# An order of work written out instruction by instruction, relu evictions over two PSUM banks, and a weight difference shared between two engines

## The chip, the cores and the metric

The kernel runs on one core of a Trainium2 chip. The metric is the time of one execution on the device, in microseconds. The core has five engines that run their own instruction streams and signal each other by semaphores: TensorE (PE, with PEld for its weight loads), VectorE (DVE), ScalarE (ACT), GpSimd (POOL) and SyncE (SP), whose queue issues DMAs here.

## The reference

Four batches of 12544 tokens of 128 channels go through an attention with 32 inducing points and then through a layer of two weight matrices, a maximum and an output matrix:

```
h   = mab(I, x)        # softmax over the 12544 tokens: 32 x 128 per batch
a   = mab(x, h)        # softmax over the 32 points: one row of 128 per token
g   = maximum(a @ w1, a @ w2)      # 50176 x 1024
out = g @ w_out                    # 50176 x 128, float32
mab(q, kv) = softmax(q @ kv.T / sqrt(128)) @ kv
```

## The kernel before, in words

A batch is 98 chunks of 128 tokens. Batch 0 is transposed by TensorE as it is loaded (the head, some 23 us); the other three are loaded by GpSimd's DMA queue while the batch before is computed (`load_x`, L223), transposed by SyncE's DMA queue (`transpose_x_dma`, L238), and reduced to h in steps that stand between the main work (`pool_scores` L393, `pool_turn` L437, `pool_accum` L442, then `small_rep`, `small_h`, `small_hwd`, `small_m1`). The last step of `pool_accum` issues the seven loads of the next batch.

The maximum is computed as max(a w1, a w2) = a w1 + relu(a (w2 - w1)). With e the unnormalised softmax of a token over 32 points and hwd = h (w2 - w1), the product for the relu has a depth of only 32, so TensorE does four of them beside each other, in four row groups. The main work on a block of up to 16 chunks, in four quarters of up to four:

- `stage` (L698): scores of the block by column-tiled products, and an exponential by ScalarE into the tile e2.
- `phase` (L1127): a visit. For up to four quarters, products of hwd and e2 (L1205) into a PSUM bank each, 512 columns a bank; with them, now and then, the products of m1 and e2 that add a w1 w_out. Then `relu_out` (L1095) evicts each bank to SBUF, by VectorE (L1107) or ScalarE (L1110) as a bit of the visit's second number says. The function can evict two neighbouring banks of one quarter at once (`holds`), which the order here never asks for.
- `final_one` (L974): one full product of 128 x 128 of relu and w_out (L989), 8 per chunk, added up in a bank per group of four chunks.
- `evict_group` (L1015): a group times the reciprocal of the softmax sum, by VectorE (L1024) or, for a few at the end, ScalarE (L1031), into one of six buffers `osbs`, which SyncE stores (L1049). The reciprocals come from `turn_e2` (L759: a DMA transpose of e2 and sums and a power by GpSimd, L776 and L780) or from `dens` (L804: small products and VectorE).

TensorE changes between full products, row tiling (the visits) and column tiling (stage, pool_scores, pool_accum). The order of this is a list of words (`ORDER`, L1229): `p4.9` is a visit of four with a mask of 9, a number is so many final products, `s` a stage, `g` a turn_e2, `x`, `c`, `t`, `a` steps of the next batch, `e`, `h`, `w`, `m` its small steps. Which bank, quarter and unit a word takes is decided while the program is built, by a model of the engines' times (`Clock`, L23) that also inserts dummy products (`dummies`, L617; `keep_busy`, L933) where it expects TensorE to wait.

In the head, w2 - w1 (`difference`, L622) is formed for columns 0 to 255 by VectorE and for the rest by GpSimd, w1 is cast to 16 bits (`cast_w1`), transposed by TensorE (`weights_2`, L635, with copies L646 and L649) and multiplied by w_out (`weights_3`, L654, L662).

The schedule within an engine is the program's order; the only waits are semaphores.

Of the kernel before, what the change touches and what calls it, by code (L numbers as in the profile page):

```python
# [16 lines left out]
INF = 1e9  # L17
# [90 lines left out]
class Quarter:  # L108


    def __init__(self, b, c0, w):
        self.b, self.c0, self.w = b, c0, w
        self.subs = {1: [1], 2: [2], 3: [2, 1], 4: [4]}[w]


class Block:


    def __init__(self, quarters, full=()):
        self.quarters = quarters  # L120
        self.width = max(qu.w for qu in quarters if qu)
        self.b = [qu.b for qu in quarters if qu][0]
        self.staged = None
        self.first = None
        self.divided = 0.0
        self.rp = None
        self.units = []
        self.done = {}
        self.relu = {}
        self.last_group = {}  # L130
        self.groups = []
        for q, qu in enumerate(quarters):
            jobs = []
            t0 = 0
            for w in qu.subs if qu else []:
                for u in range(2 * w):
                    jobs.append((q, t0, w, u))
                t0 += w
            self.units.append(jobs)
            if qu:  # L140
                self.groups.append(Group(self, [(q, t) for t in range(qu.w)], q in full))


class Group:
    def __init__(self, blk, chunks, full):
        self.blk, self.chunks, self.full = blk, chunks, full
        self.q = chunks[0][0]
        self.bank = self.ps = None
        self.started = self.linear = False
        self.order, self.parts = [], []  # L150
        for q, t0, w, u in blk.units[self.q]:
            jpb = 4 // w
            self.parts.append((t0, u))
            self.order += [(jpb * u + jj, t0 + t) for jj in range(jpb) for t in range(w)]
# [3 lines left out]
def kernel(  # L158
# [37 lines left out]
    relus = [big.tile([128, 2, 4096], F16, name=f"relus{q}", tag=f"relus{q}") for q in range(4)]  # L196
    relu1 = [big.tile([128, 1024], F16, name=f"relu1_{q}", tag=f"relu1_{q}") for q in range(2)]
    osbs = big.tile([128, NOUT, 4, C], F32, name="osbs", tag="osbs")

# [23 lines left out]
    def load_x(b, i, after=None):  # L223
        k0, n = parts[b][i]
        if after is not None:

            nc.gpsimd.tensor_copy(out=pace, in_=after)
        nc.gpsimd.dma_start(out=xn_at[b, i][:, 0:n, :], in_=xr[b, :, k0 : k0 + n, :])  # L228
        if b:
            issued = ck.on_pool(ck.pe, 0.55)  # L230
            if i == 0 and b > 1:
                ck.loading = issued - 0.55
            st[b]["ld", i] = ck.loading + 6.3 + 2.72 * i if b > 1 else 25.7 + 2.5 * i
# [4 lines left out]
    def transpose_x_dma(b, j):  # L238
        i, lo, n = turns_x[j]
        k0 = P1 * i + lo  # L240
        nc.sync.dma_start_transpose(xT_tiles[b % 2][:, k0 : k0 + n, :], xn_at[b, i][:, lo : lo + n, :])
        landed = ck.on_sp(st[b]["ld", i], "x7" if n == 7 else "x14")
        for k in range(k0, k0 + n):
            st[b]["T", k] = landed

    identity16 = consts.tile([128, 128], F16, name="identity16")
    head16 = relus[3][:, 0, :]
# [10 lines left out]
    wf = relus[0][:, 0, :].bitcast(F32)  # L258
    w1f, w2f = wf[:, 0:J], wf[:, J : 2 * J]
    w1s = relus[1][:, 0, :]  # L260
# [10 lines left out]
    with tc.manual_schedule(engines={ET.PE, ET.DVE, ET.Activation, ET.Pool, ET.SP}):  # L271

        xf = relus[2][:, 0, 0 : 256 * P1].bitcast(F32)
# [119 lines left out]
        def pool_scores(b, u):  # L393
            if u == 0:
                st[b]["es"] = smp.tile([128, NU], F32, name=f"es_{b}", tag="esu")
            bi, ps = bank([128, 512])
            ck.wait(ck.bank[bi], "p1")
# [10 lines left out]
            ck.feed(8)  # L408
            end = ck.run(0.226, "col")
# [3 lines left out]
            nc.scalar.activation(  # L413
                out=eu, in_=ps, func=AF.Exp, scale=scale, accum_out=st[b]["es"][:, u : u + 1]
            )
            ck.bank[bi] = ck.on_act(end, 0.575)
            st[b]["eu", u] = eu, ck.bank[bi]

        def pool_rest(b):

            bi, ps = bank([128, 512])
            ck.wait(ck.bank[bi], "p1")
# [8 lines left out]
            end = ck.run(0.029 * REST)  # L431
            et = etp.tile([128, P1, M], F16, name=f"et_{b}", tag="et")
            nc.scalar.activation(out=et[:, 0:REST, :], in_=ps[:, 0 : REST * M], func=AF.Exp, scale=scale)
            ck.bank[bi] = ck.on_act(end, 0.2)
            st[b]["et"] = et, ck.bank[bi]

        def pool_turn(b, u):  # L437
            eT = etp.tile([128, 8, 128], F16, name=f"eT_{b}_{u}", tag="eT", bufs=NEU)
            nc.sync.dma_start_transpose(eT, st[b]["pair", u // 2].rearrange("p v (j t) -> p (v j) t", j=4))
            st[b]["eT", u] = eT, ck.on_sp(st[b]["eu", u][1], "eT")  # L440

        def pool_accum(b, u):  # L442

            bi, ps = bank([128, 512])
            ck.wait(ck.bank[bi], "p1")
# [4 lines left out]
            if last:  # L450
                nc.vector.reduce_sum(out=acc[:, C : C + 1], in_=st[b]["es"], axis=AX.X)
                ck.on_dve(st[b]["eu", u][1], 0.1)
            eT = st[b]["eT", u][0]
            st[b]["sum", u] = True
# [12 lines left out]
            if last:  # L467
                et = st[b]["et"][0]
# [17 lines left out]
            ck.feed(64)  # L486
            end = ck.run(0.58 if last else 0.49, "col")
# [5 lines left out]
            ck.bank[bi] = ck.on_dve(end, 0.22)  # L493
            if last:
                st[b]["esrr"] = ck.bank[bi]
# [4 lines left out]
        def small_rep(b):  # L500

            bi, ps = bank([128, 512])
            ck.wait(ck.bank[bi], "p1")
            nc.tensor.matmul(out=ps[:, 0 : C + 1], lhsT=repd, rhs=st[b]["hacc"], start=True, stop=True)  # L504
            end = ck.run(0.28)
# [5 lines left out]
            ck.bank[bi] = st[b]["haccr"] = ck.on_dve(end, 0.45)  # L511

        def small_h(b):
            hT4 = smp.tile([C, 4, M], F16, name=f"hT4_{b}", tag="hT4")
            if b == 0:


                nc.vector.tensor_scalar(
                    out=hT4,
                    in0=st[0]["hps"][:, None, 0:M].broadcast_to((C, 4, M)),  # L520
                    scalar1=DOWN,
                    scalar2=None,
                    op0=ALU.mult,
                )
                st[b]["hT4r"] = ck.on_dve(st[0]["end"], 0.2)
                ck.bank[st[0]["hb"]] = st[b]["hT4r"]
                es = smp.tile([128, 1], F32, name="es_0", tag="es")
                nc.scalar.copy(out=es, in_=st[0]["eps"][:, 0:1])
                ready = ck.on_act(st[0]["end"], 0.1)
                st[b]["hT4"] = hT4.rearrange("c q m -> c (q m)")  # L530
                return es, ready
            bi, ps = bank([128, 128], F16)
            ck.wait(ck.bank[bi], "p1")
            nc.tensor.transpose(ps[:, 0:128], st[b]["h4"], identity16)
            end = ck.run(0.056)
            nc.vector.tensor_copy(out=hT4.rearrange("c q m -> c (q m)"), in_=ps[:, 0:128])
            ck.bank[bi] = st[b]["hT4r"] = ck.on_dve(end, 0.2)
            st[b]["hT4"] = hT4.rearrange("c q m -> c (q m)")
# [12 lines left out]
        def small_hwd(b, steps=(0, 1), vector=True):  # L551

            if b == 0:
                cuts = ((0, 256), (256, 512), (512, 1024))
            else:
                cuts = ((0, 512), (512, 1024))
            if 0 in steps:
                st[b]["hwd"] = smp.tile([128, J], F16, name=f"hwd_{b}", tag="hwd")
            hwd = st[b]["hwd"]
            for step in steps:  # L560
                lo, hi = cuts[step]
                w, sl = hi - lo, slice(lo, hi)
                bi, ps = bank([128, 512])
                ps = ps[:, 0:w]
                if b == 0 and step == 2:
                    n = int((w_of["w21", lo] + 0.05 - max(ck.pe, ck.bank[bi])) / 0.23)
                    if n > 0:
                        ck.wait(ck.bank[bi], "p1")
                        dummies(psall[:, bi, :], n)
                ck.wait(max(ck.bank[bi], st[b]["hT4r"], w_of.get(("w21", lo), 0.0) if b == 0 else 0.0), "p1")  # L570
                nc.tensor.matmul(out=ps, lhsT=st[b]["hT4"], rhs=w21[:, sl], start=True, stop=True)  # L571
                end = ck.run(0.215 * w / 512)
                if b == 0:
                    if vector:
                        nc.vector.tensor_scalar(  # L575
                            out=hwd[:, sl],
                            in0=ps,
                            scalar1=st[0]["rs"],
                            scalar2=1.0 / scale,
                            op0=ALU.mult,  # L580
                            op1=ALU.mult,
                        )
                    else:
                        nc.scalar.activation(out=hwd[:, sl], in_=ps, func=AF.Copy, scale=st[0]["rw"])
                elif step == 0:
                    nc.vector.tensor_copy(out=hwd[:, sl], in_=ps)
                else:
                    nc.scalar.copy(out=hwd[:, sl], in_=ps)
                if vector if b == 0 else step == 0:
                    ck.bank[bi] = ck.on_dve(end, 0.07 + w / 970.0)  # L590
                else:
                    ck.bank[bi] = ck.on_act(end, 0.06 + w / 1200.0)
                for piece in range(lo // 256, hi // 256):
                    st[b]["hw", piece] = ck.bank[bi]

        def small_m1(b):
# [726 lines left out]
```

## Time and profile before

| | us |
|---|---|
| median of 3 runs | 315.21 |
| lowest, highest | 314.35, 315.71 |
| span of the profiled execution (first to last instruction) | 312.9 |
| TensorE busy in it | 306.0 |
| ScalarE busy | 280.7 |
| VectorE busy | 273.1 |
| GpSimd busy | 122.6 |

The profiled execution is one execution of its own; its time by the device's clock is not given apart from its span, and the median of the runs lies 2.3 us above the span. Rows of groups read: line, engine, operation, output and inputs, shapes, count, then busy time, mean ns of one, and the engine's idle time before them with what ended it. Rows of a timeline read: start, duration, engine, line, operation, tiles, shapes, count. A matmul's end is modelled, so its row is longer than the time that it holds the array.

### The profile page before, as it was taken

To read this page: it belongs to the slowest core of one execution; us is meant where nothing else is said; L and a number is where in the kernel's file an instruction comes from. 1 tells how busy PE (TensorE), PEld (TensorE's weight loads), DVE (VectorE), ACT (ScalarE), POOL (GpSimd) and SP (SyncE) were. 2 spreads that over 40 slices of the span, in tenths; PEclk is the share of its full clock that TensorE was granted. 3 is DMA by queue.
4 is the path that set the end of the run, shared out by engine and by line. 5 is a ranking of instruction groups with operands and counts; after the bars stand their busy time and mean duration, and the time that the engine had idled before them with its cause. 6 is when DMAs were issued, how large, how long until landed. Compare 5 with 4: busy or idle time off the path is not lost.

```text
span 312.9 us, 12567 instructions
## 1 busy us (share of the span) xinstructions
PE 306.0 (98%) x5316; PEld 239.4 (77%) x5316; DVE 273.1 (87%) x485; ACT 280.7 (90%) x581; POOL 122.6 (39%) x183
## 2 busy tenths in 40 slices
PE   6999999999999999999999999999999999999996
PEld 2875777777877777778877887778778877788885
DVE  2458999999889999988999998999999899989894
ACT  3668999999989989999999999989999899998875
POOL 7374007910530006677500565139205743288000
PEclk9999999999999999999999999999999999999999
DMA  7999999999399999989699999993422522342223
GB/s 206 208 255 203 218 214 192 167 231 232 107 204 244 256 212 202 212 199 218 136 241 256 185 241 200 194 229 114 131 86 103 153 102 87 118 130 103 103 88 136
DMA packets 80793, 55.69 MB, mean 178 GB/s; under 512 B 62272, under 2 KB 65632, under 8 KB 80736
## 3 DMA queue, kind: packets, MB, share of 16 engines
q1 hardware_dynamic: 74768, 41.19, 56.5%
q0 software_dynamic: 5968, 13.70, 22.6%
q8 instruction: 41, 0.67, 0.9%
q14 instruction: 16, 0.13, 0.1%
HBM read 27.28 MB, written 25.69 MB: 169 GB/s over the span
## 4 chain that ended last, share of the span: by engine, by line
PE 94%; DMA 3%; DVE 1%; issue 1%; POOL 0%; ACT 0%; POOLq 0%
PE psall L989 61%; PE psall L1205 23%; DMA xn<-in_x_dram 3%; PE psall L712 2%; PE psall L458 1%; PE psall L399 1%; PE psall L309 1%; PE psall L371 1%; PE psall L325 1%; DVE relus L1107 1%; PE psall L571 1%; PE psall L504 0%; PE psall L362 0%; DVE hwd L575 0%; PE psall L819 0%
## 5 line engine op out<-in xcount | busy, mean ns | idle before, releaser
L1110 ACT ACTIVATE relus<-psall 128x512 f16<-128x512 f32 x468 | 239.2, 620 | 15.4 <-PE psall L1205 14.4
L1107 DVE TENSOR_SCALAR relus<-psall 128x512 f16<-128x512 f32 x308 | 195.5, 683 | 16.6 <-PE psall L1205 15.7
L989 PE MATMUL psall<-woutp,relus 128*128 128x128 f16 x3104 | 203.7, 220 | 0.0
L989 PEld LDWEIGHTS <-relus 128*128 128x128 f16 x3104 | 174.9, 98 | 33.1 <-issue 27.3
L1205 PE MATMUL psall<-e,hwd 32*128 32x512 f16 (+2 forms) x840 | 81.1, 362 | 0.0
L776 POOL TENSOR_TENSOR half<-ed 128x256 f32<-128x256 f16 (+2 forms) x22 | 13.4, 611 | 145.5 <-DMA ed<-e 145.5
L780 POOL TENSOR_TENSOR rd<-den,minus 128x16 f32<-128x16 f32 (+2 forms) x22 | 57.8, 2628 | 1.7
L1024 DVE TENSOR_TENSOR osbs<-psall,rd 128x512 f32<-128x512 f32 (+1 forms) x80 | 50.9, 637 | 4.3 <-PE psall L1205 1.3
L1205 PEld LDWEIGHTS <-hwd 32*128 32x128 f16 x880 | 27.9, 91 | 11.7 <-issue 2.3
L1205 PE MATMUL psall<-m,e 32*128 32x128 f16 x372 | 36.6, 216 | 0.0
L1205 PEld LDWEIGHTS <-e 32*128 32x128 f16 x372 | 22.2, 92 | 9.6 <-issue 2.0
L776 POOL TENSOR_TENSOR half<-half 128x32 f32<-128x32 f32 (+4 forms) x66 | 21.4, 324 | 5.2
L228 POOL DMA_DIRECT2D xn<-in_x_dram x32 | 17.8, 569 | 5.7 <-DMA xn<-in_x_dram 4.3
L1024 DVE TENSOR_TENSOR osbs<-psall,rp 128x512 f32<-128x512 f32 (+3 forms) x24 | 15.6, 649 | 0.5 <-PE psall L1205 0.4
L313 DVE COPY xT<-psall 128x512 f16<-128x512 f16 (+3 forms) x12 | 5.7, 485 | 8.6 <-PE psall L309 8.4
L413 ACT ACTIVATE eu<-psall 128x512 f16<-128x512 f32 x18 | 10.8, 612 | 0.3 <-PE psall L399 0.2
L725 ACT ACTIVATE e<-psall 128x512 f16<-128x512 f32 (+2 forms) x21 | 10.9, 574 | 0.1
L316 ACT COPY xT<-psall 128x768 f16<-128x768 f16 (+3 forms) x10 | 5.8, 576 | 4.6 <-PE psall L309 4.5
L309 PE MATMUL psall<-identity,xn 128*128 128x128 f16 x98 | 7.5, 219 | 1.5 <-DMA xn<-in_x_dram 1.0
L712 PE MATMUL psall<-xT,hT 128*32 128x512 f16 (+3 forms) x110 | 8.4, 362 | 0.0
L309 PEld LDWEIGHTS <-xn 128*128 128x128 f16 x98 | 5.5, 97 | 3.1 <-DMA xn<-in_x_dram 1.4
L399 PE MATMUL psall<-xT,inducingT 128*32 128x512 f16 x72 | 6.4, 381 | 0.0
(114 smaller groups left out, 129.8 us busy)
## 6 DMA issues: line engine op xcount, KB each, us to landing
out_dram<-osbs SPq DMA_DIRECT2D x90, 256.0 KB, 2.9
xn<-in_x_dram POOLq DMA_DIRECT2D x24, 448.0 KB, 9.9
out_dram<-osbs SPq DMA_DIRECT2D x10, 128.0 KB, 4.3
relus<-in_moe_w_dram POOLq DMA_DIRECT2D x4, 256.0 KB, 5.7
xn<-in_x_dram POOLq DMA_DIRECT2D x4, 224.0 KB, 10.3
xT<-xn SPq DMA_TRANSPOSE x33, 4.3
relus<-in_x_dram SPq DMA_DIRECT2D x1, 512.0 KB, 4.0
relus<-in_x_dram SPq DMA_DIRECT2D x1, 384.0 KB, 4.4
```

The source lines that it names most:

```text
L228: nc.gpsimd.dma_start(out=xn_at[b, i][:, 0:n, :], in_=xr[b, :, k0 : k0 + n, :])
L309: nc.tensor.transpose(ps[:, j, :], xn[:, g + j, :], identity16)
L413: nc.scalar.activation(out=eu, in_=ps, func=AF.Exp, scale=scale, accum_out=st[b]["es"][:, u : u + 1])
L712: nc.tensor.matmul(out=ps[32 * q : 32 * (q + 1), 128 * t : 128 * (t + n)], lhsT=hq, rhs=xT[:, c : c + n, :], start=True, stop=True, tile_p ...
L725: nc.scalar.activation(out=blk.e2[:, 0 : 128 * wd], in_=ps[:, 0 : 128 * wd], func=AF.Exp, scale=st[0]["rs"] if blk.b == 0 else scale,)
L776: nc.gpsimd.tensor_tensor(out=dst, in0=cur[:, :, 0:n], in1=cur[:, :, n : 2 * n], op=ALU.add)
L780: nc.gpsimd.tensor_tensor(out=rp[:, 0:wd, :].rearrange("p t q -> p (t q)"), in0=den[:, 0 : 4 * wd], in1=minus1[:, 0 : 4 * wd], op=ALU.pow,)
L989: nc.tensor.matmul(out=g.ps[lo:hi, 128 * c : 128 * (c + 1)], lhsT=relu[:, lo:hi], rhs=woutp[:, jb, :], start=not g.started, stop=(state["m ...
L1024: nc.vector.tensor_mul(osb[:, 0:m, :], g.ps[:, 0 : m * C].rearrange("p (s c) -> p s c", s=m), g.blk.rp[:, t0 : t0 + m, q : q + 1].broadcas ...
L1107: nc.vector.tensor_scalar(out=dst, in0=src, scalar1=0.0, scalar2=None, op0=ALU.max)
L1110: nc.scalar.activation(out=dst, in_=src, func=AF.Relu)
L1205: nc.tensor.matmul(**seq.pop(0))
```

## The change

The order is written out in full (`PLAN`): the list says for each visit which quarters it takes, into which bank each goes and which engine evicts it, and for each other step its bank. `p01+12v26a37a` is a visit: quarter 0 into bank 1 and quarter 1 into bank 2, both evicted by one VectorE instruction (`+`), quarter 2 into bank 6 and quarter 3 into bank 7, each evicted by ScalarE. `l` and `L` add the m1 products of the open or the held group, digits behind a colon give the order of the products, `o` opens a group in a bank, `d` is so many final products. The model of the engines no longer decides anything but in the head. Its description says that the list has 157 visits and that no transpose is issued during a burst of loads.

```
-    relus = [big.tile([128, 2, 4096], F16, ...) for q in range(4)]
+    slots = big.tile([128, 64, 512], F16, name="relus", tag="relus")
...
+        def relu_out(parts, vector):
+            if len(parts) == 2:
+                (a, ba), (z, bz) = [(home[1] + unit[2], bi) for home, unit, bi, _, _ in parts]
+                assert a < z and ba < bz
+                dst = slots[:, a : z + 1 : z - a, :]
+                src = psall[:, ba : bz + 1 : bz - ba, :]
+            else:
...
+            if vector:
+                nc.vector.tensor_scalar(out=dst, in0=src, scalar1=0.0, scalar2=None, op0=ALU.max)
+            else:
+                nc.scalar.activation(out=dst, in_=src, func=AF.Relu)
...
-        difference(nc.gpsimd, 512, J, 22.9, 1.25)
+        difference(nc.gpsimd, 512, 768, 22.9, 0.64)
...
+        difference(nc.vector, 768, J, 23.1, 0.34)
...
-        s p4.9 s p2.2 H1 V W p2.2 p4.2 14 m0 p3.1 4 p3.2 4 p3.3 15 p4.2 6 x1.0 2 p3.6 15 p4.8 13 p4.5 14
+        s6 p00+11a25v:12012000 s7 H2.0.0 p14v V3.6 p15v p00a p11v32v x1.0 p27a o4.1 d4.1 W6.0 p03a20a35a o7 d4
...
-        EVICT = "...000101101"
+        EVICT = "...000011010"
```

The relu results of all quarters lie in one tile, so that two banks of different quarters, neighbours or not, can go by one instruction with a stride between their halves. The list has 138 such evictions. The digit 0 or 1 of `EVICT` gives a group's eviction to VectorE or ScalarE. The steps of the head up to the second `difference` are as before, as are the loads and the number of products; the two kinds of reciprocals are shared out differently by one block.

More of the change, by code (lines that the diff above doesn't have):

```diff
@@ L412, in pool_scores, with pool_rest @@
             eu = st[b]["pair", u // 2][:, u % 2, :]
[L413 to L422, printed above, removed]
+            nc.scalar.activation(out=eu, in_=ps, func=AF.Exp, scale=scale, accum_out=st[b]["es"][:, u : u + 1])
+        def pool_rest(b, bi):
+            ps = main_bank(bi)
             for j in range(REST):
@@ L558, in small_hwd @@
+        def small_hwd(b, step, bi, scalar):
+            if step == 0:
                 st[b]["hwd"] = smp.tile([128, J], F16, name=f"hwd_{b}", tag="hwd")
[L559 to L594, printed above, removed]
@@ L933, in keep_busy @@
[L933 to L950 removed]
+        held = []
@@ new lines, with open_group, products @@
+        evicted = [0]
+        def open_group(bi, ahead=0):
+            g = groups[state["g"] + ahead]
+            assert not g.started and g.ps is None
+            g.bank, g.ps = bi, main_bank(bi)
+        def products(n, ahead=0):
+            g = groups[state["g"] + ahead]
+            home, _ = relu_home(g.blk, g.q)
+            w4 = g.n
+            more = max(0, n - (g.n * NJB - g.mm))
+            for _ in range(n - more):
+                jb, t = g.order[g.mm]
+                g.mm += 1
+                nc.tensor.matmul(
+                    out=g.ps[:, 128 * t : 128 * (t + 1)],
+                    lhsT=home[:, 128 * (jb * w4 + t) : 128 * (jb * w4 + t + 1)],
+                    rhs=woutp[:, jb, :],
+                    start=not g.started,
+                    stop=(g.mm == g.n * NJB and g.linear),
```

845 lines of the change are left out of this document (326 added, 519 removed).

## The prediction

> **What bounds the kernel now.** I read the page's shares and its chain of waits first, then what TensorE waited for, then the order of its work in a short window.
>
> ```profile
> span 312.9 us, 12567 instructions
> PE 306.0 (98%) x5316; PEld 239.4 (77%) x5316; DVE 273.1 (87%) x485; ACT 280.7 (90%) x581; POOL 122.6 (39%) x183
> PE 94%; DMA 3%; DVE 1%; issue 1%; POOL 0%; ACT 0%; POOLq 0%
> ```
>
> The chain that ended last lies on TensorE for 94%, although VectorE and ScalarE are busy for 87% and 90%. A busy engine need not delay another. Who did delay TensorE is in its list of waits (us in total, times, longest), six rows of which two below 0.5 us are left out:
>
> ```profile
> PE psall L840 <- DVE ones_q L292: 1.2, 1, 1.2
> PE psall L309 <- DMA xn<-in_x_dram: 1.0, 2, 0.8
> PE psall L662 <- DVE relus L646: 0.5, 1, 0.5
> PE psall L309 <- DVE xn L836: 0.5, 1, 0.5
> ...
> ```
>
> All of them belong to the first 27 us. After that TensorE waits for no relu eviction that this view shows. So the change can win two things only: less work on TensorE, and the few waits of the head. Relief of VectorE and ScalarE wins nothing by itself.
>
> What TensorE's work costs besides multiplying is seen in its timeline (start, duration, line, count):
>
> ```profile
> 150.56 0.40 PE L1205 MATMUL psall<-e,hwd 32*128 32x512 f16 x4
> 150.89 0.95 PE L989 MATMUL psall<-woutp,relus 128*128 128x128 f16 x14
> 151.78 0.40 PE L1205 MATMUL psall<-e,hwd 32*128 32x512 f16 x4
> 153.86 0.60 PE L1205 MATMUL psall<-e,hwd 32*128 32x512 f16 x5
> 154.41 0.84 PE L989 MATMUL psall<-woutp,relus 128*128 128x128 f16 x12
> 80.13 1.84 PE psall L989 x31
> 244.05 2.29 PE psall L989 x39
> ```
>
> The last two rows are pieces of the chain: 8 products more take 0.45 us, so one costs 56 ns. The run of 14 lasts from 150.89 to 151.78, 0.89 us, of which 14 x 56 ns are 0.78; the entry costs 0.106 us. A visit (the four-row-group products of L1205 between two such runs) of 512 columns deep takes 0.33 us, one of 1024 deep (153.86 to 154.41) 0.55; 512 columns are thus 0.22 us and its entry is 0.11 us.
>
> **The change part by part.** Counts are from the order of both built programs.
>
> *Fewer visits.* Runs in row tiling go from 165 to 158, full runs from 163 to 157, column-tiled ones from 25 to 26: 12 entries fewer, 12 x 0.106 = **-1.27 us**, all on the path. The products themselves are the same 3136 of L989 and 1262 of L1205; the columns of the deepest row group, summed over visits, grow by 256 (+0.11 us), and four small sum products go (about as much). These two cancel.
>
> *The head.* The new order takes 512 of the 1024 columns of w2 - w1 apart: 256 to GpSimd, 256 to VectorE, and scales hwd before two of the relus.
>
> ```profile
> 22.85 1.26 POOL L623 TENSOR_TENSOR w<-relus 128x512 f16<-128x512 f32 x1
> 20.84 0.89 POOL L623 TENSOR_TENSOR w<-relus 128x256 f16<-128x256 f32 x1 [0.63 <-DMA relus<-in_moe_w_dram]
> 20.71 0.42 DVE L623 TENSOR_TENSOR w<-relus 128x256 f16<-128x256 f32 x1
> 23.63 1.89 DVE L1107 TENSOR_SCALAR relus<-psall 128x512 f16<-128x512 f32 x3 [0.46 <-PE psall L1205]
> 24.16 0.61 PE L619 MATMUL psall<-warm 128*128 128x512 f16 x2
> 25.26 0.81 PE L619 MATMUL psall<-warm 128*128 128x512 f16 x3
> 25.43 0.74 DVE L575 TENSOR_SCALAR hwd<-psall,rs 128x512 f16<-128x512 f32 x1
> 26.09 0.41 DVE L646 COPY relus<-psall 128x512 f16<-128x512 f16 x1
> 26.56 0.62 PE L662 MATMUL psall<-woutp,relus 128*128 128x128 f16 x8 [0.48 <-DVE relus L646]
> ```
>
> Five dummies (512 columns, 0.22 us each) and the 0.48 stall are 1.58 us in which TensorE did nothing useful, waiting for VectorE's row of three relus, hwd and the copy L646. In the new order GpSimd ends its 256 columns at 22.85 + 0.89 = 23.74, VectorE its own, behind the scale at 23.02, near 23.6; then come on VectorE one relu (to 24.3), hwd (its product ends near 24.35, so to 25.1), one relu (25.65), the copy (26.05). L662 starts at about 26.05 in place of 26.5, and TensorE comes to it at about 26.0, since a visit and four products now stand ahead in place of the dummies. I take **-1.5 us**; no row shows the new order, so the ends are 0 (another engine ends as late as L646 did) and -2.0.
>
> *Two-bank evictions* replace 186 single ones on ScalarE by 93, and 90 on VectorE by 45.
>
> ```profile
> L1110 ACT ACTIVATE relus<-psall 128x512 f16<-128x512 f32 x468 | 239.2, 620 | 15.4 <-PE psall L1205 14.4
> L725 ACT ACTIVATE e<-psall 128x512 f16<-128x512 f32 x18 | 10.0, 613 | 0.1
> L725 ACT ACTIVATE e<-psall 128x128 f16<-128x128 f32 x2 | 0.6, 296 | 0.0
> L1024 DVE TENSOR_TENSOR osbs<-psall,rd 128x512 f32<-128x512 f32 x68 | 46.5, 683 | 2.3 <-PE psall L1205 1.1 <-ACT e L725 0.4 <-PE psall L989 0.3
> L1024 DVE TENSOR_TENSOR osbs<-psall,rd 128x256 f32<-128x256 f32 x8 | 3.3, 417 | 1.6 <-ACT osbs L1031 1.1 <-ACT relus L1110 0.6
> 149.41 4.51 ACT L1110 ACTIVATE relus<-psall 128x512 f16<-128x512 f32 x9
> ```
>
> Instructions overlap: nine on ScalarE last 4.51 us, so one follows another after (4.51 - 0.62)/8 = 0.486 us, not 0.62; on VectorE (1.89 - 0.68)/2 = 0.60. An element costs (613 - 296)/384 = 0.83 ns on ScalarE and (683 - 417)/256 = 1.04 ns on VectorE. A pair should then take a pitch of 0.486 + 0.42 = 0.91 for 0.97, and 0.60 + 0.53 = 1.13 for 1.20: 93 x 0.06 + 45 x 0.07 = 9 us freed on two engines, nothing on the path. From the row durations the pair would save more, 620 - 424 = 0.20 and 683 - 533 = 0.15; that is the upper end, 25 us; the lower end is a pair as dear as two singles. Neither moves the sum while TensorE does not wait.
>
> [...]
>
> A pair frees its banks late, though, and the new list reuses banks sooner. A single eviction needs 0.17 us from the end of streaming (a 0.38 us product row less its 0.21 of streaming), 0.62 or 0.68 for itself and some 0.05 for the signal. I laid all evictions' distances, in TensorE work at the prices above, from the last product into a bank to the next one that overwrites it, beside this need: 4 places of before fall short, by 0.14 us together, and 14 of the new list, by 0.94, the worst 0.25. The difference, **+0.8 us**, I take as added wait (bounds 0 and 1.5: queues ahead of an eviction come on top). Behind such a wait stands all of TensorE's stream, and VectorE and ScalarE wait for it in turn.
>
> *The rest.* The last eviction moves to VectorE: **-0.1** by the rows below. One block more is transposed by DMA and summed by GpSimd (39% busy, some 5 us, hidden). The order of the DMAs is a rival's matter.
>
> ```profile
> 309.86 0.37 ACT L1031 ACTIVATE osbs<-psall,rd 128x128 f32<-128x128 f32 x1 [0.62 <-PE psall L963]
> L1024 DVE TENSOR_TENSOR osbs<-psall,rd 128x128 f32<-128x128 f32 x4 | 1.2, 288 | 0.4 <-issue 0.2 <-PE psall L1205 0.2
> ```
>
> **Sum:** -1.27 - 1.5 + 0.8 - 0.1 = -2.07. The span of 312.9 becomes 310.8; around it lie 315.21 - 312.9 = 2.3 us (median less span), which stay. **Forecast 313.1 us**, 0.7% less.
>
> **The rivals.**
>
> *Given back in the evictions' queues (314.4).* In stretches of 5 us of TensorE's work, the list hands ScalarE more than 5 us (at the pitches above) in places that sum to 5.8 us, before 2.8; VectorE 4.1 against 1.3. Before, such peaks cost no wait in the list above; twice the peaks, in pairs that hold two banks, may cost 1.3 us more than I took. For it: one stretch of 10 us holds 10.8 us of ScalarE's. Against it: the totals fall. [...]
>
> *Pairs as dear as two singles (314.6).* The lower end above: ScalarE keeps its 264 us and loses the slack in a shorter span, and each of the 14 short places waits 0.1 us more: +1.5. Nothing here speaks for it but that no pair was measured.
>
> *Transposes into the loads: it does not do what it says (317, slower).* Of the change it is said that no transpose is issued during a burst of loads. The queues say otherwise.
>
> ```profile
> 84.77 3.82 POOL L228 DMA_DIRECT2D xn<-in_x_dram  x7 [0.31 <-PE psall L989]
> 86.03 20.22 SPq L1049 DMA_DIRECT2D out_dram<-osbs  x10
> 106.34 4.30 SPq L241 DMA_TRANSPOSE xT<-xn  x3
> 153.99 17.25 SPq L1049 DMA_DIRECT2D out_dram<-osbs  x8
> out_dram<-osbs SPq DMA_DIRECT2D x6, 256.0 KB, 7.8
> out_dram<-osbs SPq DMA_DIRECT2D x15, 256.0 KB, 3.0
> xT<-xn SPq DMA_TRANSPOSE x2, 8.3
> xT<-xn SPq DMA_TRANSPOSE x11, 4.3
> DMA to landing us min/median/max: 1.6/2.9/9.7
> ```
>
> Before, ten stores (one in 2.2 us) pass between the loads' issue and the first transpose, and eight in the third batch. While loads land a store takes 7.8 us, else 3.0 (windows 84 to 107 and 107 to 150); two transposes issued in the first burst took 8.3, else 4.3; the last row is all stores'. The new list lets six stores pass and four, then come four and two transposes, with stores behind them: near 97 us, ten before the loads are through. A store behind four transposes lands after 9.7 + 4 x 1.43 (the issue pitch of the row of three) = 15.4 us. There are 108 stores in 280 us and six buffers, 15.6 us a round: beyond this VectorE waits for a buffer, and TensorE for VectorE. If a transpose there costs 0.5 us more, the wait is 2 us in each of two bursts: +4. Against it: the first transpose stands behind stores that themselves land only when the loads are through.
>
> [...]
>
> **How the numbers follow.** Forecast 0.56, queues 0.22, pairs 0.10, transposes 0.12. A measurement here tells 0.5% (1.6 us) from no change: faster means below 313.6. That is the forecast's case and a little of the others, 0.58; same 0.24 (most of queues, half of pairs); slower 0.18. Range: at the low end all head and no added wait, 315.2 - 1.27 - 2.0 - 0.1 = 311.8, less 0.8 for small waits that no row names: 311.0; at the high end the transposes' 317.
>
> **What would show it.** Visits: 158 runs of products in row tiling at the same 0.33 and 0.55 us. Head: L662's successor (L607) starting near 26.0, without dummies ahead of it. Pairs: a row of 128x1024 near 1.04 us on ScalarE and 1.21 on VectorE. Short banks: waits of TensorE for relu evictions, 0.25 us at most, below 1 us in all; several us of them mean the queues. Stores landing later than 15 us and VectorE's L871 waiting for them mean the transposes. The prediction is wrong if TensorE's share falls below 97%.

## The result, and the profile after

| | before | after |
|---|---|---|
| median of 17 runs, us | 314.78 | 313.99 |
| lowest, highest | 314.35, 315.9 | 313.17, 315.54 |
| span of the profiled execution | 312.9 | 311.4 |

The ratio of after to before is 0.9977, 95% interval 0.9966 to 0.9987: 0.7 us faster, a third of the 2.07 of the sum. That the forecast of 313.1 comes within 0.9 us of 313.99 is luck: its base was the median of three runs, 315.21, and seventeen have 314.78. From that base the sum gives 312.7, 1.3 us too low.

The first lines of the page of after, with the shares of its chain:

```profile
span 311.4 us, 12499 instructions
...
PE 305.2 (98%) x5306; PEld 239.8 (77%) x5306; DVE 271.0 (87%) x443; ACT 275.5 (88%) x485; POOL 127.0 (41%) x189
...
PE 89%; DMA 6%; POOL 2%; DVE 2%; issue 1%; POOLq 0%; DVEq 0%
```

TensorE is as busy as before (98%), but its share of the chain fell from 94% to 89%. DMA and GpSimd have taken what it lost, but a link of the chain counts with its whole duration, not with the wait that it caused: 2% of the span, 6.5 us, are the landing of w1 and w2 at 14 to 21 us, ahead of the change. What the new order made TensorE wait for is in its list of waits, and it is small (us in total, times, longest; rows that before had too are left out):

```profile
PE psall L535 <- POOL w L576: 0.3, 1, 0.3
...
PE psall L430 <- DMA eT<-eu: 0.2, 1, 0.2
```

L576 is the difference w2 - w1, L535 the product hwd that reads it, L430 an accumulation that reads a DMA transpose. Neither was in the list of before. The evictions by shape (count, busy us, mean ns of one, idle time):

```profile
L902 ACT ACTIVATE relus<-psall 128x512 f16<-128x512 f32 x280 | 150.9, 608 | 14.4 <-PE psall L956 13.4 <-ACT relus L902 0.3
L900 DVE TENSOR_SCALAR relus<-psall 128x512 f16<-128x512 f32 x220 | 141.8, 684 | 15.2 <-PE psall L956 14.5
L902 ACT ACTIVATE relus<-psall 128x1024 f16<-128x1024 f32 x93 | 93.7, 1029 | 7.2 <-PE psall L956 6.7 <-ACT et L410 0.4
...
L900 DVE TENSOR_SCALAR relus<-psall 128x1024 f16<-128x1024 f32 x45 | 54.9, 1219 | 3.7 <-PE psall L956 3.4
```

A pair lasts 1.03 and 1.22 us, as forecast (1.04, 1.21).

**One execution is not the typical one.** In result and profile together, time and span lie 1.75 us apart (313.17 and 311.4; another run 314.15 and 312.4), not the 2.3 that the prediction took. So the profiled run of before, 312.9, was one of 314.7 us, a typical one, and that of after is the fastest of its seventeen. Part of the reason is in its head: the first product of the sums (of the softmax, L504, before L544) starts at 21.13 us, against 21.52 before, where nothing has been changed yet; TensorE had waited 0.4 us for loads, against 1.0. The difference of the two spans, 1.5 us, must therefore not be explained as it stands. The first experiment is the same kernel again.

**How the waits below are counted.** I add up TensorE's own work at the prediction's prices (56 ns a product, 0.105 us an entry, and for each column of the deepest row group some 0.42 ns, as dummies of 512 columns follow each other after 0.215 us: before, one lasts 0.38 us and three last 0.81) and subtract it from the real start of each product. Where this difference is flat, TensorE runs at its price; where it steps up, it waited. The price of an entry is put in here, not measured; it has an experiment of its own, the last. Two numbers are used: the *head stretch*, from the first product of the sums to the first of w1 w_out (L504 to L607, before L544 to L662), and the *waits after the head*, the growth from 30 us to the end.

### The profile page after: what moved, and what is told of

Same layout as the page of the kernel before. It is cut to its first block, busy times and chain, and to the rows that moved or that the text cites. A ratio compares the mean times of both kernels' runs of the same rounds, so it can differ in the third digit from the quotient of the medians.

```text
span 311.4 us, 12499 instructions
## 1 busy us (share of the span) xinstructions
PE 305.2 (98%) x5306; PEld 239.8 (77%) x5306; DVE 271.0 (87%) x443; ACT 275.5 (88%) x485; POOL 127.0 (41%) x189
## 4 chain that ended last, share of the span: by engine, by line
PE 89%; DMA 6%; POOL 2%; DVE 2%; issue 1%; POOLq 0%; DVEq 0%
PE psall L836 60%; PE psall L956 22%; DMA xn<-in_x_dram 3%; DMA relus<-in_moe_w_dram 2%; PE psall L644 2%; PE psall L430 1%; PE psall L385 1%; DVE relus L900 1%; DMA eT<-eu 1%; POOL xn L219 1%; POOL w L576 1%; PE psall L546 0%; PE psall L469 0%; DVE m1bd L565 0%; PE psall L852 0%
## 5 line engine op out<-in xcount | busy, mean ns | idle before, releaser
L902 ACT ACTIVATE relus<-psall 128x512 f16<-128x512 f32 (+1 forms) x373 | 234.0, 713 | 21.6 <-PE psall L956 20.1
L900 DVE TENSOR_SCALAR relus<-psall 128x512 f16<-128x512 f32 (+1 forms) x265 | 194.4, 775 | 18.9 <-PE psall L956 17.8
L956 PE MATMUL psall<-e,hwd 32*128 32x512 f16 (+2 forms) x840 | 80.2, 362 | 0.2
L697 POOL TENSOR_TENSOR half<-ed 128x256 f32<-128x256 f16 (+2 forms) x23 | 14.1, 612 | 141.8 <-DMA ed<-e 141.7
L701 POOL TENSOR_TENSOR rd<-den,minus 128x16 f32<-128x16 f32 (+2 forms) x23 | 60.7, 2639 | 1.8
L871 DVE TENSOR_TENSOR osbs<-psall,rd 128x512 f32<-128x512 f32 (+2 forms) x85 | 53.9, 636 | 4.2 <-issue 1.1
L956 PE MATMUL psall<-m,e 32*128 32x128 f16 x372 | 35.5, 217 | 0.0
L697 POOL TENSOR_TENSOR half<-half 128x32 f32<-128x32 f32 (+4 forms) x69 | 22.3, 323 | 5.4
L871 DVE TENSOR_TENSOR osbs<-psall,rp 128x512 f32<-128x512 f32 (+3 forms) x20 | 12.7, 641 | 0.4 <-PE psall L956 0.3
L385 PE MATMUL psall<-xT,inducingT 128*32 128x512 f16 x72 | 6.0, 382 | 0.0
```

The lines of the kernel that those rows point to most:

```text
L697: nc.gpsimd.tensor_tensor(out=dst, in0=cur[:, :, 0:n], in1=cur[:, :, n : 2 * n], op=ALU.add)
L701: nc.gpsimd.tensor_tensor(out=rp[:, 0:wd, :].rearrange("p t q -> p (t q)"), in0=den[:, 0 : 4 * wd], in1=minus1[:, 0 : 4 * wd], op=ALU.pow,)
L871: nc.vector.tensor_mul(osb[:, 0:n, :], g.ps[:, 0 : n * C].rearrange("p (s c) -> p s c", s=n), blk.rp[:, 0:n, q : q + 1].broadcast_to((128, ...
L900: nc.vector.tensor_scalar(out=dst, in0=src, scalar1=0.0, scalar2=None, op0=ALU.max)
L902: nc.scalar.activation(out=dst, in_=src, func=AF.Relu)
L956: nc.tensor.matmul(**seq.pop(0))
```

## The experiments

| run | median us | ratio to before, 95% | head stretch us | waits after the head us |
|---|---|---|---|---|
| before | 314.78 | | 5.04 | 3.66 |
| after, first profile | 313.99 | 0.9977 (0.9966 to 0.9987) | 4.87 | 5.05 |
| r1_same_again | 314.13 | 0.9978 (0.9964 to 0.9992) | 5.05 | 5.55 |
| r2_singles | 315.55 | 1.0021 (1.0011 to 1.0032) | 5.50 | 6.92 |
| r3_head_by_gpsimd | 314.28 | 0.9977 (0.9966 to 0.9989) | 5.26 | 5.91 |
| r4_deadlines | 314.10 | 0.9969 (0.9956 to 0.9982) | 4.70 | 5.27 |
| s1_old_order_split_head | 315.50 | 1.0015 (0.9998 to 1.0032) | 5.04 | 3.90 |
| s2_deadlines | 313.62 | 0.9967 (0.9949 to 0.9985) | 5.57 | 4.79 |
| s3_m1bd_by_gpsimd | 313.96 | 0.9980 (0.9959 to 1.0001) | 5.55 | 4.39 |
| s4_head_by_vector | 313.72 | 0.9957 (0.9942 to 0.9972) | 4.55 | 5.36 |
| t1_three_repairs | 312.96 | 0.9931 (0.9911 to 0.9952) | 4.55 | 4.38 |
| t2_cast_later | 313.08 | 0.9939 (0.9918 to 0.9961) | 4.53 | 4.63 |
| t3_banks | 312.90 | 0.9936 (0.9913 to 0.9958) | 4.56 | 4.74 |
| u1_twelve_more_entries | 316.22 | 1.0044 (1.0024 to 1.0064) | 4.84 | 4.55 |

Each ratio is to runs of the kernel before made beside that run, so ratios compare better than medians. The last two columns are of the one profiled execution. The profile of s3_m1bd_by_gpsimd shows a granted clock of 0.7 in its fourth slice of 40 (23.5 to 31.3 us), where the eight products of w1 w_out last 0.98 us, against 0.62 in after; its head is not used.

### The same kernel again

> The changed kernel once more, for a second profile. Theory A (the execution profiled first began with loads that landed early, and is not typical): TensorE's first product for the sums of the head starts near 21.5 us as in the kernel before, not at 21.1, the span is about 312.2, and from 30 us on TensorE falls behind its own work by about 1.4 us more than in the kernel before. Theory B (that execution is typical, and its 1.5 us less in the span is what the change gives): 21.1 us again and a span near 311.4.

Theory A. The sums start at 21.40, the span is 312.3, and the waits after the head exceed those of before by 1.9 us, not 1.4. The start is a matter of the execution: in the fourteen profiles it lies between 21.13 and 21.74. The timeline of its head (start, duration, engine, line; DVE is VectorE, POOL GpSimd):

```profile
21.40 0.38 PE L504 MATMUL psall<-es,relus 128*128 128x1 f32 x2 [0.18 <-ACT es L488]
...
23.02 1.14 DVE L576 TENSOR_TENSOR w<-relus 128x256 f16<-128x256 f32 x1
23.08 0.75 POOL L576 TENSOR_TENSOR w<-relus 128x256 f16<-128x256 f32 x1
...
24.21 0.39 PE L535 MATMUL psall<-w,hT 128*128 128x512 f16 x1 [0.49 <-DVE w L576]
...
26.45 0.62 PE L607 MATMUL psall<-woutp,relus 128*128 128x128 f16 x8
```

and the same place in the first profile of after:

```profile
22.73 0.42 DVE L576 TENSOR_TENSOR w<-relus 128x256 f16<-128x256 f32 x1
22.78 0.94 POOL L576 TENSOR_TENSOR w<-relus 128x256 f16<-128x256 f32 x1
...
23.77 0.38 PE L535 MATMUL psall<-w,hT 128*128 128x512 f16 x1 [0.34 <-POOL w L576]
...
26.00 0.62 PE L607 MATMUL psall<-woutp,relus 128*128 128x128 f16 x8
```

The same instruction of VectorE lasts 0.42 us in one execution and 1.14 in the other. Where it is short, GpSimd's is long (0.94), and where GpSimd's is short (0.75), VectorE's ends last. The two halves hardly run beside each other. In r1 VectorE's ends 0.33 us after GpSimd's, and 0.42 us is all that it took in the first profile; in the first profile GpSimd's ends 0.57 us after VectorE's, and 0.75 is all that it took in r1. By these durations, as an estimate, the one that ends second does most of its work after the other has ended.

### Pairs split into singles

```
-        p01+12v26a37a
+        p01v12v26a37a
```

(all 138 pairs)

> The changed kernel with every two-bank eviction split into two single ones on the same engine; order, banks and head as in the changed kernel. Theory A (pairs free about 9 us on two engines, and the list needs some of it because its peaks are higher): 0.3 to 1.0 us slower than the changed kernel. Rival (a pair frees its first bank 0.42 to 0.53 us later than a single one does, and this is what TensorE waits for): 0.3 to 0.8 us faster. Pairs off the path altogether: within 0.2 us.

Theory A, and more than it expected: 1.4 us slower than after (1.0021 against 0.9977). The page of r2 has both engines busier:

```profile
PE 306.3 (98%) x5306; PEld 239.3 (76%) x5306; DVE 274.7 (87%) x488; ACT 280.5 (89%) x578; POOL 126.8 (40%) x189
```

ScalarE has 5.0 us more than in after, 54 ns for each of its 93 pairs. VectorE has 3.7 more, of which 1.2 is the longer L576 of that execution (1.65 for 0.42); 2.5 is left, 55 ns for each of its 45. In this list a part of these 7.5 us is on the path: the waits after the head are 1.4 us longer than in r1, in many small pieces, none in the list of waits above 0.2 but for the DMA wait that r1 has too.

### The head's difference by one engine

```
-        difference(nc.gpsimd, 512, 768, 22.9, 0.64)
+        difference(nc.gpsimd, 512, J, 22.9, 1.25)
...
-        difference(nc.vector, 768, J, 23.1, 0.34)
```

> The changed kernel with all 512 columns of the second half of w2 - w1 by GpSimd, as in the kernel before; the rest unchanged. Theory A (the product of hwd waits for the difference): GpSimd needs 1.26 us in place of 0.94, the product starts 0.3 to 0.4 us later and the time grows by 0.3 to 0.4 us. Rival (the copy of the transposed w1 on VectorE sets the end of the head, and VectorE has one operation less): within 0.1 us, or 0.1 to 0.3 us faster.

```
-        difference(nc.gpsimd, 512, 768, 22.9, 0.64)
...
-        difference(nc.vector, 768, J, 23.1, 0.34)
+        difference(nc.vector, 512, J, 23.1, 0.64)
```

> The changed kernel with all 512 columns of the second half of w2 - w1 by VectorE, none by GpSimd. Theory A (VectorE and GpSimd do not run such operations beside each other: where the two halves overlap, VectorE's took 0.85 and 1.14 us instead of 0.42): VectorE alone needs about 0.8 us, the product of hwd starts 0.1 to 0.5 us earlier than in the changed kernel unless GpSimd's cast of w1 gets in its way, and the time is the same or up to 0.3 us less. Rival (the two engines really share the work): the product starts 0.3 to 0.5 us later and the time grows by as much.

GpSimd alone, from the timeline of r3:

```profile
22.99 1.26 POOL L576 TENSOR_TENSOR w<-relus 128x512 f16<-128x512 f32 x1 [0.21 <-DMA relus<-in_moe_w_dram]
...
24.31 0.38 PE L535 MATMUL psall<-w,hT 128*128 128x512 f16 x1 [0.77 <-POOL w L576]
```

VectorE alone, from that of s4 (L585 is GpSimd's cast of w1):

```profile
23.33 0.68 DVE L576 TENSOR_TENSOR w<-relus 128x512 f16<-128x512 f32 x1
23.37 1.11 POOL L585 CAST relus<-relus 128x512 f16<-128x512 f32 x1
...
24.07 0.38 PE L535 MATMUL psall<-w,hT 128*128 128x512 f16 x1
```

and both, from that of s2, in which the head is as in after:

```profile
22.88 1.66 DVE L576 TENSOR_TENSOR w<-relus 128x256 f16<-128x256 f32 x1
22.94 0.76 POOL L576 TENSOR_TENSOR w<-relus 128x256 f16<-128x256 f32 x1
...
23.62 0.64 POOL L585 CAST relus<-relus 128x512 f16<-128x512 f32 x1
...
24.60 0.39 PE L535 MATMUL psall<-w,hT 128*128 128x512 f16 x1 [1.01 <-DVE w L576]
```

VectorE makes 512 columns in 0.68 us; with GpSimd's help, half of them took it up to 1.66, past GpSimd's difference and its cast too. The split is therefore hardly shorter than GpSimd alone: stretches of 4.87, 5.05, 5.50, 4.70, 5.57 and 4.84 us, 5.09 in the mean of six, against 5.26 in one. In time, r3 and after cannot be told apart (0.9977 both), so the 0.3 to 0.4 us of r3's theory A did not show. VectorE alone gives 4.55, which is the end at 26.05 that the prediction reckoned with (26.05 - 21.52 = 4.53): s4's theory A. By the ratios (0.9957 and 0.9977) it is 0.6 us faster than after, which is at the edge of what the intervals can tell.

In these rows one of the two lasts longer than it does elsewhere: VectorE's half 1.14 and 1.66 us for 0.42, or GpSimd's 0.94 for 0.75. Which one it will be cannot be read from them: VectorE's record starts 0.05 us ahead in the first profile, where it ended first, and 0.06 us ahead in r1 and s2, where it came last. Why the two hardly run beside each other is not shown.

### The split in the old order

```
-        difference(nc.gpsimd, 512, J, 22.9, 1.25)
+        difference(nc.gpsimd, 512, 768, 22.9, 0.64)
...
+        difference(nc.vector, 768, J, 23.1, 0.34)
```

> The kernel before, with half of the last 512 columns of w2 - w1 given to VectorE as in the change; its order stays, but for dummies that move from ahead of the hwd product to ahead of w1 w_out. Theory A (the dummies went because of the new order; the split itself is worth at most 0.5 us and is spent here on other dummies): within 0.3 us of the kernel before. Rival (the split is what shortens the head, 1.5 us as predicted): 1 us or more faster.

Theory A. Although VectorE's half took only 0.41 us here, the head stretch is 5.04 as before, and the time cannot be told from that of before (1.0015). The dummies move. With r3, the new order without the split, which is as fast as after, this says that the order removes the dummies and the split does not: the new order has other work for their place.

### Transposes that land when they are needed

```
-        ... c1.5.4 a1.3.5 t1.5 p01+22a30vl
+        ... c1.5.4 t1.5 a1.3.5 p01+22a30vl
...
-        ... x3.10 o3 d18 p01+12v27a30a g20 ... g19 t3.3 d5
+        ... x3.10 t3.3 o3 d18 p01+12v27a30a g20 ... g19 d5
```

(this is s2; r4 has t3.3 a visit ahead of x3.10. In both, t2.5 also goes ahead of g13, and x2.4 to x2.6 go one or two visits earlier.)

> The changed kernel with six DMA transposes issued earlier: those of the exponentials of batches 1 to 3 whose use follows closely ahead of two reciprocals' transposes or an accumulation, and four of x of batch 2 by a visit or two. Theory A (in the list some transposes land just when TensorE needs them: 0.04, 0.04, 0.27 and 0.47 us before their use in the profile): the wait of 0.27 us at 212.9 us goes, and the time falls by 0.3 us, or by up to 0.8 if they land later in other executions. Rival (banks alone cost): within 0.1 us.

> The six transposes of r4_deadlines again, but with the last transpose of x of batch 3 kept ahead of the exponentials' transpose, where r4 put it behind and made TensorE wait 0.54 us for it (its own new wait). Theory A (transposes that land when they are needed cost 0.3 to 0.8 us an execution): no wait of TensorE for a transpose in the profile, and 0.4 to 0.8 us faster than the changed kernel. Rival (they cost nothing on average): within 0.2 us.

The timeline of after shows what is late. SP issues the transposes g20 and g19 (L688) ahead of t3.3 (L415), whose result L430 reads:

```profile
205.30 1.18 SPq L688 DMA_TRANSPOSE ed<-e  x1
...
207.20 2.42 SPq L688 DMA_TRANSPOSE ed<-e  x1
...
209.71 1.26 SPq L415 DMA_TRANSPOSE eT<-eu  x1
...
212.93 0.63 PE L430 MATMUL psall<-xn,eT 128*32 128x128 f16 x32 [0.23 <-DMA eT<-eu]
```

It was 0.2 us late here. The waits of TensorE after 27 us in r1, r3 and r4, one fence each:

```profile
PE psall L430 <- DMA eT<-eu: 0.5, 1, 0.5
```

```profile
PE psall L385 <- DMA xT<-xn: 0.3, 1, 0.3
PE psall L430 <- DMA eT<-eu: 0.2, 1, 0.2
```

```profile
PE psall L402 <- DMA xT<-xn: 0.3, 1, 0.3
```

L385 reads x2.6 near 123 us; the product started 0.04 us after its landing in after, r1 and r3 alike, the same 0.04 us as L430 after t3.3: the transpose set its time in each. By the steps of the start against the work, beyond those of s2 at the same places, the two cost 0.02 + 0.30 us in after, 0.21 + 0.61 in r1 and 0.71 + 0.31 in r3. From issue to landing they took nearly the same each time (x2.6 4.60, 4.67 and 4.54 us, t3.3 3.17, 3.11 and 3.12). What differed is when SP came to issue them: the issue of g19 ahead of t3.3 alone lasts 2.42, 2.85 and 2.56 us. r4 took these two away and made another (x3.10 behind t3.3, 0.5 us), so its time is no test. s2 has neither of the two, and its waits after the head are 4.79, 0.26 less than in after and 0.76 less than in r1; its median is 0.4 us less than that of after, and the intervals overlap, so the runs do not show the gain. One transpose for the batch-1 accumulation near 82 us stayed at the edge (some 0.05 us in s2, 0.25 in s4 and t2). So theory A holds by the traces, for the place and for 0.3 to 1.0 us, and how much of it a given execution pays varies; the time of s2 alone does not show it.

### VectorE's queue at 230 us

```
-            if b == B - 1:
-                outs = [(m1bd[32 * q : ..., q, :], ...) for q in range(4)] + outs
...
+            for q in range(4 if b == B - 1 else 0): nc.gpsimd.tensor_copy(out=m1bd[...], in_=m1[...])
```

> The changed kernel, but the four small copies of batch 3's m1 into m1bd, 1.18 us of VectorE just before the wait at 230.46 us, are made by GpSimd from SBUF. Theory A (VectorE's relus stand behind these copies and the next visit needs the bank): the wait of 0.34 us goes, 0.3 us faster. Rival (the bank is reused too soon by the list whatever VectorE does): the wait stays at 0.2 us or more.

After, then s3:

```profile
227.73 1.18 DVE L565 CAST m1bd<-psall 32x128 f16<-32x128 f32 x4
...
229.13 1.28 DVE L900 TENSOR_SCALAR relus<-psall 128x512 f16<-128x512 f32 x2
...
229.94 0.39 PE L956 MATMUL psall<-e,hwd 32*128 32x512 f16 x2
...
230.46 0.40 PE L956 MATMUL psall<-e,hwd 32*128 32x512 f16 x4
```

```profile
230.26 1.32 POOL L567 COPY m1bd<-m 32x128 f16<-32x128 f16 x4 [11.63 <-DVE m L565]
...
230.87 1.29 DVE L900 TENSOR_SCALAR relus<-psall 128x512 f16<-128x512 f32 x2 [0.68 <-PE psall L956]
...
232.13 0.39 PE L956 MATMUL psall<-e,hwd 32*128 32x512 f16 x2
...
232.36 0.38 PE L956 MATMUL psall<-e,hwd 32*128 32x512 f16 x3
```

In after the visit's first two products start at 229.94, and the rest stand until 230.46, 0.05 us after the second relu ends (229.13 + 1.28 = 230.41). In s3 VectorE is idle before those relus (0.68), and the gap is 0.23 us, the work's own. The step of 0.34 us is gone: theory A by the trace. In after, r1, r3, r4, s2, s4 and u1 this step stands alike; in s3 and in the three t runs, which have the same copies by GpSimd, it is gone. The medians do not tell it (313.96 and 313.99).

### The repairs together, and one short place

```
+        load_x(1, 3)
         cast_w1(1)
...
-        p06a37v p31a x1.9 p02v13a24a
+        p06a37v p33a x1.9 p04v11a22a
```

(the first for t2 and t3, the second for t3)

> The changed kernel with the three repairs of s2 (six transposes earlier), s3 (m1bd by GpSimd) and s4 (the second half of w2 - w1 by VectorE alone) together. Theory A (each removes a wait of its own: transposes 0.3 to 0.8 us, VectorE's queue at 230 us 0.35, head 0.2 to 0.5): 0.9 to 1.5 us faster than the changed kernel, some 312.7 us. Rival (the waits pass on to the next late thing): 0.4 us or less faster, with other waits of TensorE in their place.

> As t1_three_repairs, and GpSimd issues one load of x ahead of its cast of w1, so that VectorE forms the difference while GpSimd moves no data. Theory A (VectorE's operation lasts 0.7 us when GpSimd is still, and up to 1.7 when GpSimd happens to come first): the difference lasts 0.7 us, and the time is that of t1_three_repairs or up to 0.3 us less, with less spread. Rival (the later cast holds up the transposes of w1 and with them the end of the head): 0.2 to 0.5 us slower than t1_three_repairs.

> As t2_cast_later, with three banks exchanged at one of the short places of the list: two quarters that went into banks 3 and 4, 0.83 us of TensorE's work after the last product into them, go into 1 and 2, 1.9 and 2.1 us after it, and one quarter that waited for bank 1 takes bank 3 instead, 1.04 us after. Theory A (the short places cost about their shortfall, 0.11 us here): TensorE's falling behind between 50 and 60 us shrinks by about 0.1 us; the time changes by less than can be told. Rival (what is lost there is something else): no change of it.

t1 is 2.2 us faster than before (0.9931) and 1.4 faster than after: theory A, and the fastest kernel here with t2 and t3. Its page:

```profile
span 310.8 us, 12494 instructions
...
PE 304.4 (98%) x5306; PEld 239.2 (77%) x5306; DVE 270.1 (87%) x439; ACT 275.1 (89%) x485; POOL 127.3 (41%) x192
```

No wait of TensorE after 27 us is listed in it. That the three repairs together win is clear of noise; how the 1.4 us divide among them is shown by the traces alone. t2 did not differ in time, nor was its spread smaller: VectorE's difference lasted 0.68 us in s4 and t1 already, where it was GpSimd's cast that lasted longer (1.11 us, against 0.64 in t2). t3 went against theory A: with the short place removed, the waits from 38 to 58 us are 0.58 us instead of 0.22. The step near 53 us stayed as it was, and a new stop came at 55.30, for a relu of ScalarE that began more than a microsecond after its product. A list of short distances, taken place by place, does not tell where TensorE waits. ScalarE came to that relu at the end of a row of relus back to back, which points to the queue in front of ScalarE; this was not tried further.

### Twelve entries more than needed

```
-        d21 p07a11v32al p06v14+25a d11
+        d20 p07a11v32al d1 p06v14+25a d11
```

(twelve times)

> The changed kernel with twelve of its double visits taken apart by one final product between the halves, taken from the run ahead of them: the same products, columns and evictions, 24 entries of TensorE into a mode more. Theory A (an entry costs 0.105 us on the path): 24 x 0.105 = 2.5 us slower than the changed kernel, some 316.5, less up to 0.5 that TensorE would have waited for evictions anyway. Rival (entries are largely hidden by the pipeline, and so the 12 that the change saved were worth less than 1.27 us): 0 to 1.2 us slower.

Theory A: 2.1 us slower than after (1.0044 against 0.9977), with 0.7 us either way by the two intervals. The trace shows the price at each place: between the same products of u1 and after, two entries more take 0.21 to 0.22 us at eight of the twelve places, and 0.16 to 0.32 at the others. At that price the 24 cost some 2.6 us; by the same count the waits after the head are 0.5 to 1.0 us shorter than in after and r1. That the evictions got time is the likely reason, not a tested one.

## Why the prediction was wrong

Two steps failed. The larger is the added waits after the head: +0.8 in the sum, +1.4 and +1.9 in the two profiles of after. The sum had only bank distances in it; it put the order of the DMAs at nothing ("a rival's matter") and left queues ahead of an eviction to the upper bound of 1.5. Transposes issued late cost 0.3 and 0.8 us in these two profiles, and relus behind small copies 0.34. The smaller is the head: -1.5 in the sum, -1.3 and -1.1 in the profiles, because two halves of one operation on two engines were priced as if they ran beside each other. The sum beside the two profiles of after, against the one of before:

| step | predicted | first profile | second profile |
|---|---|---|---|
| fewer mode entries | -1.27 | -1.27 | -1.27 |
| head | -1.5 | -1.3 | -1.1 |
| added waits after the head | +0.8 | +1.4 | +1.9 |
| last eviction | -0.1 | 0 | 0 |
| loads ahead of the head (no part of the change) | | -0.4 | -0.1 |
| sum | -2.07 | -1.6 | -0.6 |
| difference of the spans | | -1.5 | -0.6 |

The row of the entries is the same in all columns because the waits are counted with that price; what tests it is u1.

- **What bounds the kernel**: right. TensorE is busy for 98% of the span in before, after, r1, r2, s3, t1 and u1, and holds 94% of the chain in before and 89% in after.
- **Fewer mode entries**: right. An entry costs what the rows gave: 0.21 to 0.22 us for two at most of the places in u1, and 2.1 us slower for 24, less waits that went.
- **The head**: this step failed: "GpSimd ends its 256 columns at 22.85 + 0.89 = 23.74, VectorE its own, behind the scale at 23.02, near 23.6". So the hwd product could start 2.2 us after the sums; it started 2.64 and 2.81 us after them, and 2.33 in s4. Six dummies went (1.15 us, five of them in the stretch) and other work, 0.95 us, took their place in it; but the stretch was to shrink to 4.53 us beside, and it did not shrink in the mean (5.09 for 5.04). The -1.3 and -1.1 are the 1.15 and the change of the waits up to 30 us (-0.16, +0.02). The 0.42 us of VectorE came from a row in which GpSimd's 256 columns took 0.89 us beside it; GpSimd's 512 columns took 1.26, so 0.89 for half of them already held a wait, and r1 and s2 have 0.75 and 0.76 for it. Both rows stood in the prediction; that one engine's gain there was the other's loss was not read. With VectorE alone the predicted end is met.
- **Two-bank evictions**: the size was right, 9 us by the pitch against 7.5 measured. "Nothing on the path" was wrong in this list: without the pairs it is 1.4 us slower, close to the +1.5 of the rival that priced them as dear as singles.
- **Short bank distances, +0.8**: what is left of the waits without transposes and m1bd is 5.05 - 3.66 - 0.32 - 0.34 = 0.73 in the first profile and 5.55 - 3.66 - 0.82 - 0.34 = 0.73 in the second. The sum agrees with the 0.8; t3 says that the places do not, so the agreement is not shown to be for the reason given, and what makes up the 0.73 stays open.
- **What the sum lacked**: 0.34 us for relus behind 1.18 us of small copies on VectorE, a case of the rival on the evictions' queues (which had 1.3 in peaks everywhere), and 0.3 to 1.0 us of transposes that land when they are needed. The prediction looked for transposes in the bursts of loads, where the cost was nothing: from 84 to 112 us TensorE falls behind its work by 0.28 us in after and by 0.45 before. The list does issue transposes there, against its description; the loads of this burst land up to 105.5 us. That burst in after (SP's issues, then the median us to landing):

```profile
84.97 11.82 SPq L885 DMA_DIRECT2D out_dram<-osbs  x6
96.90 1.20 SPq L688 DMA_TRANSPOSE ed<-e  x1
...
99.62 7.74 SPq L227 DMA_TRANSPOSE xT<-xn  x3
```

```profile
out_dram<-osbs SPq DMA_DIRECT2D x6, 256.0 KB, 7.8
...
xT<-xn SPq DMA_TRANSPOSE x4, 5.9
```

  Stores land there as late as before (median 7.8 us, the longest 9.3, where 15 were feared), and VectorE waited for no buffer (no wait of L871 for a store is listed). The transposes that cost something stand elsewhere, at 123 and 213 us, behind other transposes in SP's queue. "The order of the DMAs is a rival's matter" left them out of the sum.
- **The last eviction**: 308.05 to 308.66 after, 309.61 to 310.23 before, from the start of the last product to the end of the last eviction: 0.61 and 0.62 us, nothing gained. VectorE's eviction is shorter (0.29 for 0.37) and starts later after the product (0.32 for 0.25).
- **The share of TensorE**, 98%, stayed above the 97% named as the sign of error; it could not show what was wrong.
- **With the three repairs** the sum comes out: from before to t1, whose sums start at the same time (21.50 for 21.52), the head gives -1.6 and the added waits are +0.7, beside the -1.27 of the entries. The span is 310.8, as the prediction had it, but in a kernel that has no late transpose, no copies ahead of the relus and no split in the head.

These rows belong to the last eviction: the last product of before (its eviction is in the prediction), then the end of after.

```profile
309.61 0.22 PE L963 MATMUL psall<-m1bd,e 128*128 128x128 f16 x1
...
308.05 0.22 PE L852 MATMUL psall<-m1bd,e 128*128 128x128 f16 x1
308.37 0.29 DVE L871 TENSOR_TENSOR osbs<-psall,rd 128x128 f32<-128x128 f32 x1 [1.02 <-PE psall L852]
```

## What to carry to other kernels

When an order is written out by hand, each DMA whose landing a bounding engine reads needs a due time with slack for the queue it is issued in; here one that cost 0.30 us in one execution cost 0.61 in another of the same kernel, because the queue came to it later. Work shared between two engines is shared only if rows show both at their short durations at the same time; here VectorE's 0.42 us came with GpSimd's 0.94, and GpSimd's 0.75 with VectorE's 1.14. Before a difference of two spans is explained, look at a point ahead of the change: if it differs there already (here 21.13 us against 21.52), that part belongs to the execution.

## What the runs showed of the hardware

- VectorE's subtraction of two fp32 operands in SBUF (256 columns) lasted from 0.41 us (s1, GpSimd's half beside it 0.99) to 1.66 (s2, GpSimd's half 0.76); in r2, s2 and s3 it ended 0.28 to 0.30 us after the second of two instructions of GpSimd in a row.
- GpSimd's cast of 512 columns lasted 0.60 us with no difference of VectorE beside it (r3), and 0.62 (r2) to 1.11 (s4) with one.
- An entry of TensorE into full or row-tiled products cost some 0.107 us: two of them 0.21 to 0.22 us at eight of twelve places of u1. A column-tiled run of 512 columns took 0.33 us from its start to that of the next run, and so did the row-tiled run of 512 columns behind it (after: 22.37, 22.70, 23.03).
- The same DMA transpose took nearly the same time from issue to landing in after, r1 and r3 (within 0.13 us); its lateness came from when SP's queue reached it.
- Two banks evicted by one instruction took some 55 ns less of an engine's busy time than by two (r2: 54 on ScalarE, 55 on VectorE).
